# Scores of the first batch: one product of 64 rows per head, masks of a unit ahead of its products

## The chip, the core and the metric

The kernel runs on one core of a Trainium2 chip. TensorE (PE, with its weight loads shown apart as PEld), VectorE (DVE), ScalarE (ACT), GpSimd (POOL) and SyncE (SP, which issues the transfers) run side by side and wait for each other by semaphores. The metric is the device time of one execution in microseconds; several executions of a kernel are given by their median.

## What is computed

Sparse attention over 4 batches and 8 heads, then two feed-forward blocks with a softmax-like layer in the second. Only the attention's scores are touched here:

```python
scores = scale * np.matmul(q, k.transpose(0, 1, 3, 2))         # B, H, S, D = 4, 8, 576, 64
mask_local = (rel >= 0) & (rel < 32)                           # heads 0 to 3
mask_strided = (rel >= 0) & (pos[None, :] % 32 == pos[:, None] % 32)   # heads 4 to 7
scores = np.where(masks[None, :, :, :], scores, -1e9)
attn = softmax(scores); x = attn @ v                           # then x (2304 x 512) goes on:
h = x @ w_in; g = P(h) / (Q(h) + 1e-6); x = g @ w_out          # first block, 2048 wide
h = x @ w_in2; ...; out = ln @ w_out2                          # second block, 1024 wide
```

## The kernel before

**Units.** The attention of one batch is cut into 12 units of two heads each. Units 0 to 5 are local (blocks of 96 queries by 127 keys, two blocks per unit), units 6 to 11 strided (blocks of 126 x 126, 108 x 108 and, in units 8 and 11, a single 108 x 108). A unit has a score product and a mask product for each block of each head: 4 of each, or 2. The two heads of a pair lie one above the other in a tile `qkb`: head 0 of the pair in rows 0 to 63, head 1 in rows 64 to 127. The keys stand there twice, once with zeros in the other head's rows, so that a product over all 128 rows gives one head's scores. For the first batch the third and fourth pair lie in `ws` and `wo_l` (lines of `load_qk`).

**A score.** `scores_head` first adds the mask as a bfloat16 product with the identity (`ident_b`, `mask_b`; it starts the accumulation) and then the float32 product of queries and keys on top. In the first batch (`attn_scores2`) a unit has one PSUM bank for each head: even units `bank0` and `bank1`, odd units the two halves of the pair `banks4`. Later batches (`attn_scores1`) put both heads into one bank, with the same `scores_head`.

**After the scores** come, for a unit, two maxima on DVE (`attn_softmax`), four exponentials on ACT (`attn_exp`), the sum and reciprocal on DVE, the scaling on POOL (`attn_norm`), four transposes on PE (`attn_tp`), an eviction on ACT, the products with V (`attn_pv`: one head writes output rows 0 to 63, the other 64 to 127, so each uses half of the columns of TensorE; the four products of a unit are recorded and mostly stand in the order first head, first head, second head, second head, but in one unit of a later batch, at 251 and 255 us, the planner has put the two heads' products apart, two and two), and the split of the result into two float16 parts, `xs` or `tail`, on ACT and DVE.

**Beside it** run the weight conversions. `w_in` and `w_out` come as 64-bit floats in 8 chunks of 1 MB each; DVE turns a chunk into float32 with three integer instructions on 128 x 1024 elements (`w_conv`), ACT squares it for a scale, PE sums the squares (`ssq`), and ACT and DVE split it into two float16 parts (`w_split`: `wi_h`, `wi_l`, `wo_h`, `wo_l`). When all of `w_in` is converted, `w_pmax` gives `pmax_wi`, and `g_scale` works out the scales of the first block (`pg`, `ih`, `ac`) in some 15 small POOL instructions; the first block's element work (`A`, `p`, `q`, `L`) waits for these.

**What sets the order.** All instructions are recorded, and `Order` lays them out: every engine's instructions get one fixed order, by a planner that goes by costs (`cost`) and due times, over the whole kernel at once. In `cost`, a float32 product with 64 output rows counts half of one with more. All instructions are issued in `emit`, so the profile gives nearly all of them line L413, and they are told apart by their tiles.

Of the kernel before, what the change touches and what calls it, by code (L numbers as in the profile page):

```python
# [17 lines left out]
STRIDE = 32  # L18
# [6 lines left out]
LQ = 96  # L25
LW = LQ + STRIDE - 1
NLB = S // LQ
TPR = S // STRIDE
RG = [7, 7, 6, 6, 6]
RS = [0, 7, 14, 20, 26]  # L30
NSG = len(RG)
QP = S + STRIDE
# [79 lines left out]
class Order:  # L112
# [86 lines left out]
    def cost(self, op):  # L199
        def size(x):  # L200
            n = 1
            for d in x.shape[1:]:
                n *= d
            return n
# [3 lines left out]
        out = (op.outs or op.ins)[0][1]  # L208
        n = max([size(out)] + [size(x) for _, x in ins])
        op.port, op.land = False, 0.0  # L210
        if op.eng == "PE":
            f32 = op.ins[-1][1].dtype == F32
            op.t = size(out) / 2400 + 0.0025
            if op.call == "transpose":
                op.t = 2 * op.t
            elif f32:
                op.t = 2 * size(out) / 2400 + 0.055 if out.shape[0] == 64 else 4 * op.t + 0.03
            op.work = size(out) * op.ins[0][1].shape[0] * out.shape[0] / 16384 * ((2 if op.call == "transpose" else 4) if f32 else 1)
        elif op.eng == "ACT":
            op.t = 0.08 + n * 0.00088 + (0.05 if psum else 0) + (0.09 if "accum_out" in op.k else 0)  # L220
            op.t += 0.08 if n > 300 and hasattr(op.k.get("bias"), "shape") else 0
            op.t = max(op.t, 0.11)
        elif op.eng == "DVE":
            sb = [x for b, x in ins if not b]
            two = op.call in ("scalar_tensor_tensor", "tensor_tensor")
            fast = not two and not psum and op.call == "tensor_scalar"
            op.t = 0.07 + n / (1900 if fast else 960) + (0.08 if "accum_out" in op.k else 0)
            op.t += 0.06 * sum(1 for b, x in op.ins if size(x) == 1)
            op.port = n >= 8 and (len(sb) >= 2 if two else fast)
        elif op.eng == "POOL":  # L230
            two = op.call == "tensor_tensor"
            h = two and out.dtype == F16
            op.t = 0.1 + n * (0.002 if h else 0.0022 if two else 0.00125 if op.call == "tensor_scalar" else 0.001)
            op.t += 0.1 if op.call == "tensor_scalar" and n < 32 else 0
            op.port = bool(ins)
        else:
            op.t = 0.55
            rows, run = min(x.shape[0] for _, x in op.ins + op.outs), min(x.ap[-1][1] for _, x in op.ins + op.outs)
            op.land = n * self.SIZE[out.dtype] * out.shape[0] / (170e3 if op.call != "dma_start" else 240e3 if rows == 64 else 300e3 if run <= 128 else 375e3) * 1.12
# [177 lines left out]
def kernel(ctx: ExitStack, tc: tile.TileContext, qk, v, w_in, w_out, ab, w_in2, w_out2, gln, out):  # L417
# [240 lines left out]
    def unit_info(u):  # L658
        if u < 6:
            p, j = divmod(u, 3)  # L660
            return p, True, [2 * j, 2 * j + 1]
        p, j = divmod(u - 6, 3)
        return 2 + p, False, [[0, 1], [2, 3], [4]][j]

    def blk_dims(local, i):
        if local:
            return LQ, LW
        n = RG[i] * TPR
        return n, n

    at = {}

    def mask_of(local, i, nq, nk):
        return mask_b[0:nq, 2 if not local else 0 if i == 0 else 1, 0:nk]
# [12 lines left out]
    def attn_scores2(b, u):  # L687
        if u % 2 == 0:
            at[b, u] = [psum("h", bufs=2), psum("h", bufs=2)]
        else:  # L690
            t = psum("y", (128, 1024))
            at[b, u] = [t[:, 0:512], t[:, 512:1024]]
        for hh in range(2):
            scores_head(b, u, hh, at[b, u][hh], 0)

    def attn_scores1(b, u):
        t = psum("a", bufs=2)
# [719 lines left out]
```

## Time and profile before

| | us |
|---|---|
| median of 3 runs | 756.23 |
| lowest, highest | 755.44, 756.89 |
| the profiled execution | 757.08 |
| its span | 755.3 |

| engine | busy share of the span | instructions |
|---|---|---|
| PE | 93% | 5406 |
| DVE | 72% | 1114 |
| ACT | 65% | 1155 |
| POOL | 47% | 380 |

The profiled execution is 0.85 us above the median, and 1.8 us of it lie outside its span. The busy shares are means over two very different parts: the first 130 us, in which the weights are converted and the first batch's attention is made, and the rest, in which PE has hardly a gap. The chain that ended last is 84% PE by its share of the span. TensorE's clock has two levels, 1.2 and 2.4 GHz; the granted clock is given as 0.50 or 1.00.

### The profile page before, as it was taken

Reading aid. Unit: us, or ns where it says so; the run is one execution under the profiler, and the core shown is the slowest. Engines: PE = TensorE matmul, PEld = TensorE weight load, DVE = VectorE, ACT = ScalarE, POOL = GpSimd, SP = SyncE. Lnnn points to the kernel's source line nnn. Section 1 sums busy time; section 2 is a strip of 40 time slices with the busy share of each in tenths; the row PEclk is TensorE's granted clock in tenths of the full one; section 3 lists DMA queues with packets and bytes.
Section 4 is the critical chain, followed back from the end, with each engine's and each line's share of the span. In section 5 each row is a group of like instructions: output and inputs, shape, how many; then the busy total and the mean of one; then the engine's idle time right before and its main releaser. Section 6 shows DMA issues by size and latency. Waiting matters only on the chain.

```text
span 755.3 us, 14378 instructions
## 1 busy us (share of the span) xinstructions
PE 699.9 (93%) x5406; PEld 531.7 (70%) x5406; DVE 547.1 (72%) x1114; ACT 489.8 (65%) x1155; POOL 353.0 (47%) x380
## 2 busy tenths in 40 slices
PE   3975368999999999999999999999999999999997
PEld 3763256898888888787777777777776776765443
DVE  6789899689968997787775577576565766644571
ACT  2787558869789679977766676465655646533451
POOL 3233659755689667776434343533534334320000
PEclk9575569999999999999999999999999999999999
DMA  9996801133421321303202010110201011011244
GB/s 270 312 273 167 223 1 34 35 131 127 132 65 60 117 72 34 83 16 62 62 15 43 1 43 1 44 33 10 43 1 43 21 23 43 1 43 43 56 78 103
DMA packets 68101, 55.98 MB, mean 74 GB/s; under 512 B 39616, under 2 KB 56000, under 8 KB 67520
## 3 DMA queue, kind: packets, MB, share of 16 engines
q1 hardware_dynamic: 68032, 55.07, 28.1%
q8 instruction: 42, 0.69, 0.4%
q14 instruction: 27, 0.22, 0.1%
HBM read 40.90 MB, written 4.72 MB: 60 GB/s over the span
## 4 chain that ended last, share of the span: by engine, by line
PE 84%; DVE 7%; ACT 3%; POOL 2%; issue 2%; DMA 1%; SPq 0%; ACTq 0%; DVEq 0%
PE bank L413 46%; PE banks L413 38%; POOL tiny L413 2%; DMA qkb<-in_qk_dram 1%; DVE tiny L413 1%; DVE wi_l L413 1%; DVE T L413 1%; DVE gtb L413 1%; DVE wo_l L413 1%; ACT e L413 1%; DVE p L413 1%; ACT p L413 1%; ACT wo_h L413 0%; DVE bank L413 0%; ACT ysb L413 0%
## 5 line engine op out<-in xcount | busy, mean ns | idle before, releaser
L413 PE MATMUL bank<-xs,wi_h 128*128 128x256 f16 x1152 | 200.0, 278 | 4.0 <-DVE xs L413 2.5
L413 PE MATMUL bank<-xs,wi_l 128*128 128x256 f16 x576 | 159.9, 278 | 1.3 <-DVE wi_l L413 1.3
L413 PE MATMUL banks<-gtb,wo_h 128*128 128x256 f16 x896 | 151.4, 273 | 0.9 <-ACT ysb L413 0.9
L413 PEld LDWEIGHTS <-wi_h 128*128 128x128 f16 x1248 | 124.2, 100 | 30.7 <-issue 4.1
L413 PEld LDWEIGHTS <-wo_h 128*128 128x128 f16 x1152 | 111.7, 98 | 22.1 <-issue 0.9
L413 POOL TENSOR_SCALAR q<-A,aba 128x512 f32<-128x512 f32 x72 | 66.2, 919 | 129.4 <-ACT A L413 129.2
L413 PE MATMUL banks<-gtb,wo_l 128*128 128x256 f16 x448 | 122.1, 273 | 1.7 <-ACT ysb L413 1.7
L413 DVE SCALAR_TENSOR_TENSOR p<-p,ac,bank 128x512 f32<-128x512 f32 x144 | 106.5, 744 | 3.1 <-ACT A L413 0.7
L413 POOL TENSOR_TENSOR gtb<-p,gtb 128x512 f16<-128x512 f32 x56 | 66.8, 1194 | 75.2 <-ACT gtb L413 75.2
L413 DVE TENSOR_TENSOR p<-p,bank 128x512 f32<-128x512 f32 x72 | 49.2, 684 | 69.2 <-ACT p L413 68.7
L413 POOL TENSOR_TENSOR q<-q,A 128x512 f32<-128x512 f32 x72 | 91.7, 1273 | 4.3
L413 PE MATMUL banks<-wi_h,ysb 128*128 128x512 f16 x288 | 90.7, 379 | 0.0
L413 ACT ACTIVATE A<-bank,ih 128x512 f32<-128x512 f32 x72 | 49.6, 689 | 50.8 <-PE bank L413 48.0
L413 DVE SCALAR_TENSOR_TENSOR q<-q,bank 128x512 f32<-128x512 f32 x72 | 49.3, 685 | 34.7 <-ACT bank L413 25.3
L413 PEld LDWEIGHTS <-ysb 128*128 128x128 f16 x432 | 42.1, 98 | 43.8
L413 PE MATMUL bank<-wo_h,T 128*128 128x512 f16 x224 | 70.6, 379 | 0.0
L413 PEld LDWEIGHTS <-wi_l 128*128 128x128 f16 x576 | 57.3, 99 | 12.3 <-issue 3.1
L413 ACT ACTIVATE gtb<-p 128x512 f16<-128x512 f32 x56 | 35.3, 630 | 41.0 <-DVE p L413 41.0
L413 PEld LDWEIGHTS <-wo_l 128*128 128x128 f16 x576 | 56.4, 98 | 7.6 <-issue 0.8
L413 ACT ACTIVATE L<-q 128x512 f32<-128x512 f32 x72 | 45.3, 630 | 24.3 <-POOL q L413 24.0
L413 ACT ACTIVATE p<-bank,ac 128x512 f32<-128x512 f32 x72 | 56.0, 777 | 3.0 <-PE bank L413 3.0
L413 PEld LDWEIGHTS <-T 128*128 128x128 f16 x336 | 32.9, 98 | 34.6
(257 smaller groups left out, 1429.0 us busy)
## 6 DMA issues: line engine op xcount, KB each, us to landing
qkb<-in_qk_dram SPq DMA_DIRECT2D x28, 304.0 KB, 4.6
out_dram<-ot SPq DMA_DIRECT2D x18, 256.0 KB, 2.4
wo_h<-in_w_out_dram SPq DMA_DIRECT2D x4, 1024.0 KB, 5.4
wo_l<-in_w_out_dram SPq DMA_DIRECT2D x4, 1024.0 KB, 7.8
vl<-in_v_dram SPq DMA_DIRECT2D x4, 768.0 KB, 5.1
wi_h<-in_w_in_dram SPq DMA_DIRECT2D x3, 1024.0 KB, 5.4
wi_l<-in_w_in_dram SPq DMA_DIRECT2D x3, 1024.0 KB, 4.9
wo_h<-in_w_in_dram SPq DMA_DIRECT2D x3, 1024.0 KB, 17.3
```

The lines of the kernel that those rows point to most:

```text
L413: getattr(self.real[op.eng], op.call)(*[real(x) for x in op.a], **{k: real(x) for k, x in op.k.items()})
```

## The change

`attn_scores2` no longer calls `scores_head`. It writes the masks of all blocks and both heads of a unit first and then the score products, block by block, the two heads after each other. Each product takes only its head's 64 rows of queries and keys (`t[r, ...]`), so the first head's products use rows 0 to 63 of TensorE and the second head's rows 64 to 127; they write to the two banks that the unit had before. The zeros that made 128-row products possible are still written and loaded. `cost` now also counts a float32 product over 64 rows as half. `attn_scores1`, and with it the later batches, stay as they were in the code.

```diff
-                op.t = 2 * size(out) / 2400 + 0.055 if out.shape[0] == 64 else 4 * op.t + 0.03
+                op.t = 2 * size(out) / 2400 + 0.055 if min(out.shape[0], op.ins[0][1].shape[0]) == 64 else 4 * op.t + 0.03
...
-        for hh in range(2):
-            scores_head(b, u, hh, at[b, u][hh], 0)
+        p, local, ids = unit_info(u)
+        t = qk_t[b, p]
+        nq, nk = blk_dims(local, ids[0])
+        o = [[at[b, u][hh][0:nq, 128 * jj:128 * jj + nk] for hh in range(2)] for jj in range(len(ids))]
+        for jj, i in enumerate(ids):
+            for hh in range(2):
+                PE.matmul(o[jj][hh], lhsT=ident_b[0:nq, 0:nq], rhs=mask_of(local, i, nq, nk), start=(jj == 0), stop=False, skip_group_check=True)
+        for jj, i in enumerate(ids):
+            for hh in range(2):
+                r = slice(64 * hh, 64 * hh + 64)
+                q0 = i * LQ if local else RS[i] * TPR
+                k0 = (1 + hh) * QP + (i * LQ + 1 if local else STRIDE + RS[i] * TPR)
+                PE.matmul(o[jj][hh], lhsT=t[r, q0:q0 + nq], rhs=t[r, k0:k0 + nk], start=False, stop=True, skip_group_check=True)
```

Since the planner orders everything, the order moves on all engines, up to about the middle of the kernel; from there on PE's order (its last 4909 rows) is the same as before. Three places follow.

**PE, the scores of units 0 and 1**, the first of the kernel (`bank0` and `bank1` belong to unit 0, `banks4` to unit 1; `e0`, `ones_f` is a small sum for V). Before:

```order
L413 MATMUL bank2_88<-e0_92,ones_f_78 128x128
L413 MATMUL bank0_86<-qkb0_126 96x127
L413 LDWEIGHTS ident_b_79
L413 MATMUL bank0_86<-mask_b_80,ident_b_79 96x127
L413 MATMUL bank0_86<-qkb0_126 96x127
L413 MATMUL bank1_87<-qkb0_126 96x127
L413 LDWEIGHTS ident_b_79
L413 MATMUL bank1_87<-mask_b_80,ident_b_79 96x127
L413 MATMUL bank1_87<-qkb0_126 96x127
```

Now:

```order
L413 MATMUL bank2_88<-e0_92,ones_f_78 128x128
L413 MATMUL bank0_86<-qkb0_126 96x127 x2
L413 MATMUL bank1_87<-qkb0_126 96x127 x2
L413 MATMUL banks4_90<-qkb0_126 96x127 x4
L413 LDWEIGHTS ident_b_79
L413 MATMUL bank0_86<-mask_b_80,ident_b_79 96x127
```

All eight masks of the two units now stand ahead of the small sum, and the eight products follow each other, by head in twos.

**PE, unit 4** (`bank0`, `bank1`) with what lies between (`bank3` takes transposes, `ident`; `vl` marks the products with V). Before:

```order
L413 MATMUL bank0_86<-qkb1_127 96x127
L413 LDWEIGHTS ident_b_79
L413 MATMUL bank0_86<-mask_b_80,ident_b_79 96x127
L413 MATMUL bank0_86<-qkb1_127 96x127
L413 LDWEIGHTS ident_b_79
L413 MATMUL bank1_87<-mask_b_80,ident_b_79 96x127
L413 MATMUL bank1_87<-qkb1_127 96x127
L413 MATMUL bank3_89<-q1_98,vl0_111 64x96 x4
L413 MATMUL bank2_88<-ident_77,p2_96 127x96 x4
```

Now:

```order
L413 MATMUL bank0_86<-mask_b_80,ident_b_79 96x127
L413 MATMUL bank0_86<-qkb1_127 96x127
L413 MATMUL bank2_88<-q0_97,vl0_111 64x96 x4
L413 MATMUL bank0_86<-qkb1_127 96x127
L413 LDWEIGHTS ident_b_79
L413 MATMUL bank1_87<-mask_b_80,ident_b_79 96x127
L413 MATMUL bank3_89<-ident_77,p1_95 127x96 x3
L413 LDWEIGHTS ident_b_79
L413 MATMUL bank1_87<-mask_b_80,ident_b_79 96x127
L413 MATMUL bank1_87<-qkb1_127 96x127 x2
L413 MATMUL bank3_89<-ident_77,p1_95 127x96
```

The two heads' products of the unit no longer stand together: products with V, masks and transposes have come between them. So it is in most units: from unit 3 on the 32 score products stand in 20 separate pieces, and in one piece alone are both heads.

**DVE, around the instruction `pg0` that waits for the POOL work of `g_scale`**, and `p0`, the first element work of the first block. Before:

```order
L413 TENSOR_SCALAR pg0_136<-tiny_113 128x1
L413 SCALAR_TENSOR_TENSOR wi_l_68<-wo_l_70,scl_wi_116,wi_h_67 128x4x256
L413 TENSOR_SCALAR tiny_113<-pg0_136 128x1
L413 TENSOR_REDUCE tiny_113<-vs0_112 128x1
L413 TENSOR_REDUCE gm2_85<-bank2_88 128x1
L413 TENSOR_TENSOR tiny_113<-tiny_113 128x1
L413 TENSOR_SCALAR pat_wo_115<-bank3_89 128x2
L413 TENSOR_SCALAR gb0_138<-tiny_113 128x1
L413 TENSOR_SCALAR scl_wo_117<-pat_wo_115 128x2
L413 TENSOR_TENSOR gm2_85<-gm2_85 128x1
L413 TENSOR_TENSOR p0_94<-p0_94,bank0_86 128x512
L413 SCALAR_TENSOR_TENSOR wo_l_70<-T1_103,scl_wo_117,wo_h_69 128x16x64
```

Now:

```order
L413 SCALAR_TENSOR_TENSOR wi_l_68<-wo_l_70,scl_wi_116,wi_h_67 128x4x256
L413 TENSOR_SCALAR pg0_136<-tiny_113 128x1
L413 TENSOR_SCALAR inv_wi_118<-pat_wi_114 128x8
L413 TENSOR_SCALAR tiny_113<-pg0_136 128x1
L413 TENSOR_REDUCE tiny_113<-vs0_112 128x1
L413 TENSOR_REDUCE gm2_85<-bank3_89 128x1
L413 SCALAR_TENSOR_TENSOR wo_l_70<-T1_103,scl_wo_117,wo_h_69 128x16x64
L413 SCALAR_TENSOR_TENSOR wo_l_70<-T0_102,scl_wo_117,wo_h_69 128x16x64
L413 TENSOR_TENSOR tiny_113<-tiny_113 128x1
L413 TENSOR_SCALAR pat_wo_115<-bank2_88 128x2
L413 TENSOR_TENSOR p0_94<-p0_94,bank0_86 128x512
```

One weight split (into `wi_l`) now stands ahead of `pg0`, and two (into `wo_l`) ahead of `p0`, instead of behind them.

## Rows read from the trace of the kernel before

**Rows 1.** Busy us (instructions) by stretch; granted PE clock, DMA share, GB/s.

```profile
core 0: us, PE busy (x) PEld busy (x) DVE busy (x) ACT busy (x) POOL busy (x), PEclk, DMA share, GB/s
19.40:43.30 23.90, 22.76 (x127) 19.81 (x127) 17.04 (x39) 16.75 (x66) 7.04 (x5) 0.50 1.05 311
43.30:53.50 10.20, 6.69 (x63) 5.42 (x62) 9.46 (x25) 9.73 (x34) 3.24 (x3) 1.00 1.09 246
53.50:97.90 44.40, 21.91 (x107) 14.86 (x108) 41.62 (x75) 27.59 (x60) 20.73 (x22) 0.50 0.71 186
101.30:111.50 10.20, 6.48 (x31) 4.75 (x32) 10.13 (x19) 4.84 (x10) 9.10 (x10) 0.50 0.00 0
131.00:755.00 624.00, 617.11 (x4883) 465.50 (x4883) 433.26 (x887) 404.68 (x916) 288.26 (x297) 1.00 0.20 51
```

**Rows 2.** PE in order of time: start, duration, operation; waits in brackets.

```profile
11.62 0.74 PE L413 MATMUL bank<-qkb 128*96 128x127 f32 x2 [1.04 <-ACT qkb L413]
...
15.75 0.31 PE L413 MATMUL bank<-mask_b,ident_b 96*96 96x127 bf16 x1
...
20.75 0.74 PE L413 MATMUL banks<-qkb 128*96 128x127 f32 x2
21.29 0.31 PE L413 MATMUL banks<-mask_b,ident_b 96*96 96x127 bf16 x1
21.39 1.10 PE L413 MATMUL banks<-qkb 128*96 128x127 f32 x4
...
30.18 0.31 PE L413 MATMUL banks<-mask_b,ident_b 96*96 96x127 bf16 x1
30.29 0.68 PE L413 MATMUL banks<-qkb 128*96 128x127 f32 x2
30.77 0.31 PE L413 MATMUL banks<-mask_b,ident_b 96*96 96x127 bf16 x1
31.01 0.91 PE L413 MATMUL bank<-q,vl 127*64 127x96 f32 x8
31.85 1.17 PE L413 MATMUL bank<-ident,p 96*127 96x96 f32 x4
...
43.15 0.46 PE L413 MATMUL bank<-ws 128*108 128x108 f32 x2
...
52.07 0.40 PE L413 MATMUL banks<-wo_l 128*108 128x108 f32 x2
```

**Rows 3.** PE later on, at 2.4 GHz: the products with V of three pieces.

```profile
244.30 0.56 PE L413 MATMUL bank<-pts,vl 127*64 127x96 f32 x8
...
251.47 0.55 PE L413 MATMUL bank<-pts,vl 127*64 127x96 f32 x4
...
254.67 0.54 PE L413 MATMUL bank<-pts,vl 127*64 127x96 f32 x4
```

**Rows 4.** ACT in order of time: second head pair scaled, first element work.

```profile
20.02 0.68 ACT L413 ACTIVATE qkb<-qkb 128x576 f32<-128x576 f32 x1
...
84.37 0.69 ACT L413 ACTIVATE A<-bank,ih 128x512 f32<-128x512 f32 x1 [1.35 <-POOL ih L413]
```

**Rows 5.** What DVE waited for between 12.5 and 48 us: total, times, longest.

```profile
DVE tiny L413 <- PE banks L413: 3.9, 7, 1.7
DVE tiny L413 <- PE bank L413: 2.2, 3, 1.5
DVE tiny L413 <- ACT p L413: 2.1, 2, 1.8
DVE pat_wi L413 <- PE bank L413: 0.7, 1, 0.7
```

**Rows 6.** DVE in order of time, unit 11's maximum, then around pg and p.

```profile
56.02 0.26 DVE L413 TENSOR_REDUCE tiny<-banks 108x1 f32<-108x108 f32 x1
...
80.48 0.17 DVE L413 RECIPROCAL tiny<-tiny 128x2 f32<-128x2 f32 x1 [0.16 <-POOL tiny L413]
...
82.93 0.15 DVE L413 TENSOR_SCALAR pg<-tiny 128x1 int32<-128x1 int32 x1 [1.01 <-POOL tiny L413]
83.00 1.28 DVE L413 SCALAR_TENSOR_TENSOR wi_l<-wo_l,scl_wi,wi_h 128x1024 f16<-128x1024 f32 x1
...
87.83 0.69 DVE L413 TENSOR_TENSOR p<-p,bank 128x512 f32<-128x512 f32 x1 [1.50 <-ACT p L413]
88.44 2.48 DVE L413 SCALAR_TENSOR_TENSOR wo_l<-T,scl_wo,wo_h 128x1024 f16<-128x1024 f32 x2
```

**Rows 7.** POOL in order of time, the work of g_scale.

```profile
71.24 9.05 POOL L413 TENSOR_SCALAR tiny<-tiny,aba 128x1 f32<-128x1 f32 x3
...
82.59 0.31 POOL L413 TENSOR_SCALAR tiny<-tiny,aba 128x1 f32<-128x1 f32 x1
```

**Rows 8.** PE in order of time, the last long waits ahead of the full stretch.

```profile
101.89 0.59 PE L413 MATMUL bank<-ssq_wo,ones_f 128*128 128x2 f32 x2 [2.77 <-ACT e L413]
105.61 0.26 PE L413 MATMUL bank<-mask_b,ident_b 96*96 96x127 bf16 x1 [3.13 <-DVE vmax L413]
```

**Rows 9.** Page, transfers: count, KB each, median us from issue to landing.

```profile
wo_h<-in_w_in_dram SPq DMA_DIRECT2D x3, 1024.0 KB, 17.3
```

## What was predicted

> **What bounds the kernel now.** I read the stretches by busy time first, then PE in order of time, then what DVE and PE waited for. From 131 us on PE has 617.11 us of work in 624 [rows 1], at the full clock, and its order from the middle on is unchanged; nothing that the change does can be gained there. The question is when PE comes into that stretch. Ahead of it the bound changes. From 19.4 to 43.3 us PE is busy for 22.76 of 23.90 us at a granted clock of 0.50, while DVE has 17.04 of work [rows 1], and what DVE waits for is mostly PE's scores: 3.9 + 2.2 us of its waits up to 48 us end with a bank that PE filled, 2.1 with exponentials on ACT, 0.7 with a sum for the weight scales [rows 5]. From 53.5 to 97.9 us DVE is the bound, 41.62 of 44.40 us, with PE busy for half the time [rows 1]. DVE's waits there are few: 0.16, 1.01 and 1.50 us around the scales of the first block [rows 6]. The last long waits of PE stand at 101.89 and 105.61, 2.77 and 3.13 us; the second is released by a maximum on DVE [rows 8]. So the change pays through DVE: fewer waits for scores before 48 us, or a better order later.
>
> **The price of a product.** At 1.2 GHz a float32 product over 128 rows comes every 0.59 us with its mask (30.18 to 30.77), of which 0.11 are the mask (30.18 to 30.29). A second product without a mask between costs 0.42 (four passes last 1.10, two last 0.68) [rows 2]. So putting masks first saves 0.06 a product.
>
> **What 64 rows bring** is not in the trace, but its twin is: the products with V use half of the columns, one half per head. A piece with both heads, eight passes, takes 0.56 us; a piece of four passes of one head takes 0.55 and 0.54 [rows 3]. Two heads side by side cost what one costs, and one head alone gains nothing. The bounds of a 64-row product are therefore 0.42 us alone and 0.21 in a pair; I take these by what stands beside it in the new order, not by the planner's half.
>
> In that piece the passes overlap although the program has first head, first head, second head, second head. The Trainium skill says otherwise (TensorE: Matmul & The Clock Gate, Part 3, The mechanism): matrix products start and end in strict program order. By that rule only the two passes at a border between the heads would overlap; the first eight products would take 2.7 us instead of 1.7, and the later sum would be 0.2 more. The trace does not agree: by it one head's four passes and both heads' eight last equally long.
>
> **What a change of shape costs.** From a mask to the products with V it is 0.24 us (30.77 to 31.01) instead of 0.11, so 0.13 to go in. The group lasts 0.84 (31.01 to 31.85) [rows 2], its four products in pairs should take 0.64 (0.42 x 96/127 = 0.32, twice), so 0.20 more for its first product and going out. I take 0.33 for a visit, the nearest row, for half of the rows too; the bounds are nothing and 0.33.
>
> **The sum, part by part.**
>
> 1. Units 0 and 1. Eight products from 11.62 to 15.75 become four pairs: 1.7 + 0.3 = 2.0 instead of 4.1 us, and their masks are done before. Worth 0 at the end: unit 3's products need the second pair's queries, which ACT scales from 20.02 on [rows 4], and they begin at 20.75 [rows 2]. That cover is the transfer; without it 2 us would be gained on PE.
>
> 2. Units 3 to 11, from 20.75 on. 32 products with their masks were 32 x 0.59 = 18.9. Now 32 x (0.42 + 0.11) = 17.0, plus 20 visits x 0.33 = 6.6, less 0.4 for the one pair that meets, less 6 x 0.13 = 0.8 for visits that border on products with V: 22.4. PE has 3.5 us more to do at 1.2 GHz, 2.4 of it up to unit 8 (22 products, 14 visits). Before, PE also waited there twice for about 0.5; the new order fills that. For DVE I count both ways: units 4 to 6 follow with fewer interruptions by the first units' transposes, units 7 to 11 are later. DVE has other work in its queue behind most of those maxima, and a weight split now stands among them. I take +0.5 us, from -1 to +3.
>
> 3. DVE from 80 to 90 us. The split into `wi_l` (1.28) now stands ahead of the wait for `pg`, the two into `wo_l` (2.48) ahead of that for `p` [rows 6]. These waits were 1.01 and 1.50, with 0.16 before. If the splits cover them whole, -2.7; if POOL only becomes later by the same, 0: its three small instructions at 71.24 took 9.05 us while DVE was full, one at 82.59 0.31 [rows 7], so a split in front of the wait can hold POOL up. ACT's halves of the splits also come first. I take -2.0.
>
> 4. PE from 101.89 to 105.61. The maximum that ended the 3.13 us [rows 8] now stands ahead of three splits on DVE. What is late next are sums of `w_out` and element work, and DVE and ACT stay nearly full. I take -0.5, from -3 to 0.
>
> 5. Transfers. The queue of SP keeps its order of loads up to `w_out`; a chunk of `w_in` lands 17.3 us after its issue [rows 9], so DVE can't run far ahead. Nothing, with a loss of up to 1 when the last units' scores free `wo_l` later. The later batches' code is the same, and their order is only reshuffled: 0, within 1.
>
> Net -2.0: 757.08 - 2.0 = 755.1 for an execution like the profiled one, which stood 0.85 above the median: **754.2**. The bounds of its own parts make 752.5 to 756.3.
>
> **The rivals.**
>
> *Slower: half the clock where it was full.* From 43.3 to 53.5 us PE had the full clock, after a stretch of dense 128-row products, and 6.69 us of work [rows 1]. With half the rows, and transposes and products with V between them, the clock may stay at 1.2 GHz. That work then takes up to 6.7 us more, and with part 2 unit 11's scores end at 57.5 to 59 instead of 52.5 (52.07 and 0.40 [rows 2]). The maximum of unit 11 on DVE came at 56.02 [rows 6], so some 3.5 us are covered; beyond that DVE waits, with the conversions of the last `w_in` chunks behind it, and `pmax_wi`, the POOL chain and the first block's work wait for those. Price: 1.5 to 3 in place of the 0.5 of part 2, and half of part 3 lost: +2.5, 758.7 us (757 to 761). For it: PE was nearly full from 19.4 to 43.3 at 0.50 all the same, so a busy PE alone does not bring the clock. Against it: DVE's own work fills much of that time.
>
> *Nothing reaches the end.* POOL delays `pg` and `p` by what the splits take, and parts 2 and 4 cancel: 756.2, within 1.
>
> *The halves overlap everywhere, and a visit costs nothing.* If the two row halves run beside masks and transposes too, the 6.6 us go, and the waits for scores of rows 5 go with them, up to 6.1; the landing of the chunks leaves perhaps 4.5 beyond the forecast: 749.7 (748.5 to 752). The 0.13 into the products with V speaks against it.
>
> *The change does not do what it says*: by the order, 10 of 44 products find a partner. That is part of the forecast, and the reason why it is small.
>
> **How the numbers follow.** Forecast 0.45, slower rival 0.25, nothing 0.17, overlap everywhere 0.13. About 0.2% (1.5 us) is what a measurement of this kernel can tell from no change: faster means below 754.7, slower above 757.7. The forecast has its likeliest time half a microsecond below the first of these; I give 0.28 of its 0.45 to faster, 0.16 to no difference and 0.01 to slower. The slower rival gives 0.20 and 0.05 to no difference; nothing 0.02, 0.13 and 0.02; overlap 0.13 to faster. Sums: faster 0.43, same 0.34, slower 0.23. The range 750.5 to 759.0 leaves out half of the overlap case and the upper third of the slower one, under 0.2 in all. Since both signs are held, the forecast's own range stands beside it: 752.5 to 756.3.
>
> **What the profile after would show.** Eight products of units 0 and 1 in about 2 us with passes in pairs, and unit 3 still at about 20.7 (part 1). Pieces of one head at 0.42 a product, with 0.13 and more before and after (part 2); unit 8's scores 1 to 2 us later than 43.6 (43.15 and 0.46 [rows 2]). DVE's waits at `pg` and `p` gone or short, and the first block's `A` not later than 84.37 [rows 4] (part 3). PE's wait at 105.61 shorter, and the full stretch some 2 us earlier. Wrong would be: the clock at 0.50 through 43 to 53 us with DVE waiting for units 9 to 11 (slower); pieces of one head at 0.21 a product, or no 0.13 (faster).

## The result, and the profile after

| | us, median (lowest to highest) |
|---|---|
| before | 756.56 (755.44 to 759.08, 4 runs) |
| after | 764.58 (763.96 to 764.92, 4 runs) |
| ratio | 1.0089, 95% interval 1.0061 to 1.0116 |
| the profiled execution of after, its span | 763.96, 762.0 |

The change makes the kernel 0.9% slower: 8.0 us, outside the predicted range of 750.5 to 759.0 and away from the forecast of 754.2. About two thirds of that are the half rows themselves. Their price on TensorE I had nearly right and then let vanish behind DVE; with the clock that they cost I had them as a rival, at half of the size. The last third I had put at nothing: the new order of the later batches.

Two stretches of [rows 1] in after, in the same columns, and one more:

```profile
19.40:43.30 23.90, 23.53 (x113) 17.91 (x113) 15.60 (x35) 16.33 (x60) 7.85 (x6) 1.00 1.05 311
43.30:53.50 10.20, 9.05 (x46) 6.82 (x45) 7.92 (x20) 8.31 (x26) 2.69 (x2) 1.00 0.95 201
111.50:124.40 12.90, 7.94 (x52) 6.27 (x51) 12.90 (x28) 11.11 (x18) 12.34 (x15) 0.74 0.03 6
```

The PEclk of 1.00 in the first two rows is no reading. The clock's record of this execution begins only at 83 us, and what lies before it is printed as 1.00. The level there is read from durations: four transposes of 96 columns take 1.17 us at 20.44, and a unit's products with V 0.91 at 44.40, as they did at 0.50 before (31.85 and 31.01) [rows 2]; at 2.4 GHz the products with V took 0.56 [rows 3]. So PE worked at 1.2 GHz through the whole of the first two rows, and was busy for 32.58 of 34.10 us.

PE of after in order of time, as in [rows 2]: the eight products of units 0 and 1, unit 3, unit 8, unit 11, then two waits of many after 100 us:

```profile
11.18 1.17 PE L413 MATMUL bank<-qkb 64*96 64x127 f32 x8 [0.98 <-ACT qkb L413]
12.13 1.16 PE L413 MATMUL banks<-qkb 64*96 64x127 f32 x8
...
19.77 0.73 PE L413 MATMUL banks<-qkb 64*96 64x127 f32 x2 [2.52 <-ACT qkb L413]
20.44 1.17 PE L413 MATMUL bank<-ident,p 96*127 96x96 f32 x4
...
43.78 0.69 PE L413 MATMUL bank<-ws 64*108 64x108 f32 x2
44.40 0.91 PE L413 MATMUL bank<-q,vl 127*64 127x96 f32 x8
...
58.72 0.69 PE L413 MATMUL banks<-wo_l 64*108 64x108 f32 x2
...
118.14 0.59 PE L413 MATMUL bank<-ssq_wo,ones_f 128*128 128x2 f32 x2 [2.01 <-ACT wo_h L413]
...
304.27 0.38 PE L413 MATMUL bank<-xs,wi_h 128*128 128x256 f16 x2 [1.48 <-DVE p L413]
```

The first eight products go in pairs: sixteen passes from 11.18 to about 13.1 us (the second unit's start 0.95 us after the first's), where before the products and the masks between them took 4.1. Unit 11's last score ends at 59.4 instead of 52.5. What DVE waited for from 12.5 to 48 us, as in [rows 5], and after them unit 11's last maximum and `pmax_wi`:

```profile
DVE tiny L413 <- PE banks L413: 5.7, 3, 2.4
DVE tiny L413 <- PE bank L413: 2.5, 3, 1.3
```

```profile
63.35 0.25 DVE L413 TENSOR_REDUCE tiny<-banks 108x1 f32<-108x108 f32 x1
...
75.49 0.14 DVE L413 TENSOR_SCALAR pmax_wi<-tiny 128x1 f32<-128x1 f32 x1
...
84.67 1.28 DVE L413 SCALAR_TENSOR_TENSOR wi_l<-wo_l,scl_wi,wi_h 128x1024 f16<-128x1024 f32 x1
87.04 0.15 DVE L413 TENSOR_SCALAR pg<-tiny 128x1 int32<-128x1 int32 x1 [1.09 <-POOL tiny L413]
```

The same maximum and `pmax_wi` in before, and then the first `A` in after:

```profile
57.32 0.25 DVE L413 TENSOR_REDUCE tiny<-banks 108x1 f32<-108x108 f32 x1
...
70.64 0.14 DVE L413 TENSOR_SCALAR pmax_wi<-tiny 128x1 f32<-128x1 f32 x1
```

```profile
87.68 0.69 ACT L413 ACTIVATE A<-bank,ih 128x512 f32<-128x512 f32 x1
```

DVE's waits for banks grow from 6.1 us [rows 5] to 8.2 up to 48 us, and to 9.8 up to 62 us, where before none were added. Unit 11's last maximum came at 57.32 before and comes at 63.35, `pmax_wi` at 75.49 instead of 70.64, the first `A` at 87.68 instead of 84.37 [rows 4]. DVE did not wait for that last maximum, whose score had ended 3.9 us earlier (59.4): it was late already, by its waits for the units ahead. More is lost later. Two stretches of before, with the columns of [rows 1]:

```profile
111.50:124.40 12.90, 10.60 (x95) 8.76 (x94) 12.73 (x25) 10.21 (x30) 11.16 (x13) 1.00 0.12 30
131.00:450.00 319.00, 318.00 (x2793) 261.78 (x2793) 251.50 (x546) 249.79 (x648) 197.76 (x214) 1.00 0.23 65
```

and the second of them in after:

```profile
131.00:450.00 319.00, 314.57 (x2775) 259.09 (x2774) 248.98 (x538) 247.70 (x643) 202.60 (x213) 1.00 0.24 63
```

From 131 to 450 us PE now has 4.4 us of gaps where it had 1.0, and the clock that came for good at 111.5 us comes at 124.4.

### The profile page after: what moved, and what is told of

It is laid out like the page before. It is cut to its first block, busy times and chain, and to the rows that moved or that the text cites. A ratio compares the mean times of both kernels' runs of the same rounds, so it can differ in the third digit from the quotient of the medians.

```text
span 762.0 us, 14374 instructions
## 1 busy us (share of the span) xinstructions
PE 710.7 (93%) x5406; PEld 535.4 (70%) x5406; DVE 548.6 (72%) x1114; ACT 492.0 (65%) x1155; POOL 363.6 (48%) x380
## 4 chain that ended last, share of the span: by engine, by line
PE 86%; DVE 6%; ACT 3%; DMA 2%; POOL 1%; issue 1%; SPq 1%; ACTq 0%; DVEq 0%
PE bank L413 47%; PE banks L413 38%; DMA qkb<-in_qk_dram 2%; POOL tiny L413 1%; DVE p L413 1%; DVE wo_l L413 1%; DVE T L413 1%; DVE gtb L413 1%; DVE tiny L413 1%; ACT ysb L413 1%; SPq L413 1%; DVE wi_l L413 1%; DVE xs L413 0%; ACT e L413 0%; ACT wi_h L413 0%
## 5 line engine op out<-in xcount | busy, mean ns | idle before, releaser
L413 POOL TENSOR_SCALAR q<-A,aba 128x512 f32<-128x512 f32 x72 | 64.1, 890 | 130.7 <-ACT A L413 130.4
```

The lines of the kernel that those rows point to most:

```text
L413: getattr(self.real[op.eng], op.call)(*[real(x) for x in op.a], **{k: real(x) for k, x in op.k.items()})
```

## The experiments

Each was run beside the kernel before, whose median there was 756.4 to 756.6, and 758.7 once (beside the kernels with repeated masks). Read them for two questions: what do the half rows cost, and what does the new order cost? In the first group the order of all engines is kept, instruction for instruction, and only the product is exchanged.

**Before's order, half rows.** The recorded product stays as it was, so the planner does the same; what is issued is the half.

```diff
+            op = PE.matmul(oo, lhsT=t[:, q0:q0 + nq], rhs=t[:, k0:k0 + nk], ...)
+            if b == 0:
+                r = slice(64 * hh, 64 * hh + 64)
+                op.k.update(lhsT=t[r, q0:q0 + nq], rhs=t[r, k0:k0 + nk])
```

> The order of the kernel before on every engine, instruction for instruction, with each product of the first batch over its head's 64 rows. Each product stands right behind its mask, which takes 96 or more rows, so each of the 44 is a change in and out. Theory 'rows': 44 x 0.35 = 15 us more PE work at 1.2 GHz ahead of 60 us, of which PE's waits there hide a few: 764 to 772. Theory 'order': within 2 us of before, 755 to 758.

769.45 us, ratio 1.0156 (1.0118 to 1.0193). PE of this kernel in order of time:

```profile
31.19 0.34 PE L413 MATMUL banks<-mask_b,ident_b 96*96 96x127 bf16 x1
31.46 0.73 PE L413 MATMUL banks<-qkb 64*96 64x127 f32 x2
32.12 0.34 PE L413 MATMUL banks<-mask_b,ident_b 96*96 96x127 bf16 x1
...
34.17 1.17 PE L413 MATMUL bank<-ident,p 96*127 96x96 f32 x4
```

Mask and product repeat every 0.93 us (31.19 to 32.12); with 128 rows they repeated every 0.59 [rows 2]. A half-row product between full-row work costs 0.34 us more than a full one, which is the 0.33 of the prediction. `A` comes at 96.86 us, 12.5 later than before, and that difference stands unchanged to the end. The 44 visits are worth 44 x 0.34 = 15 us on PE. The 12.5 are not theirs alone, though: no change of the clock is recorded in this execution before 109 us, so the full clock that before had from 43.3 to 53.5 us [rows 1] is gone too, and no run tells the two apart in this order.

**After's order, 128 rows.** The same in reverse, on the changed kernel.

> The changed kernel's order on every engine, instruction for instruction, but each score product over all 128 rows again. Theory 'rows' (the price is that of the 64-row products themselves: going in and out of half rows, some 0.35 us for each of about 22 pieces at 1.2 GHz, and the clock that comes back at 124 us instead of 111): almost all of the 8.0 us is gained back, 756 to 758 us, unit 11's scores end at about 53 us, the full stretch's clock is back at about 112 us. Theory 'order' (the price is that of the new order, in which maxima, transposes and splits stand elsewhere): 762 to 765, unit 11's scores still at 56 or later. In both, the first eight products take about 3.4 us instead of 2.

783.78 us. This says nothing on the rows. PE waited once, for a transfer:

```profile
15.97 0.41 PE L413 MATMUL bank<-qkb 128*96 128x127 f32 x2
45.08 0.74 PE L413 MATMUL bank<-qkb 128*96 128x127 f32 x2 [28.71 <-DMA qkb<-in_qk_dram]
```

The last product of unit 2 belongs to the second head. Over 128 rows it also reads the first head's rows (against zeros), and in the changed order these are already the target of the next batch's load. Half rows had made that order possible. The next kernel keeps half rows in units 2 and 5, the last readers of a pair:

> The changed kernel's order, with products over 128 rows in all units but 2 and 5 (the last readers of a pair's tile, whose second head's products must not touch the first head's rows, since those are reloaded for the next batch first). Against the changed kernel this takes away 24 or more of the half-row products and leaves every order. Theory 'order': the early delay (first element work A at 87.7 instead of 84.4) and the 3.3 us of new gaps after 131 us both stay, 763 to 766. Theory 'rows': the gaps after 131 us stay, the early 3.7 us go, 760 to 762.

758.18 us (756.09 to 761.70), ratio 1.0022 (0.9997 to 1.0047). Exchanging the rows in the changed order gives back 6.4 of the 8 us, so theory "order" falls as the main cause. The time is below the range of theory "rows" as well: in the profiled execution `A` comes at 80.4 us, earlier even than in before. That the later gaps stay, as both theories had it, holds: PE is busy for 314.22 of the 319 us from 131 to 450 us, as in after. And the ten runs fall into two groups, six up to 759.2 and four from 761.0 to 761.7; the experiments on the clock, below, bear on that.

**Other orders.** Does any new order cost? Four kernels: masks first with full rows (the planner counts them in full and makes its own order), the change with the product counted in full, and the kernel before with one number of the planner moved by a hair.

```diff
-                op.t = ... else 4 * op.t + 0.03
+                op.t = ... else 4 * op.t + 0.031        (reshuffle_a)
-    EARLY, PEARLY, SLACK = 0.1, ...
+    EARLY, PEARLY, SLACK = 0.101, ...                   (reshuffle_b)
```

> Only the first half of the change: the masks of a unit first, the products still over 128 rows and counted by the planner in full, so its own new order. Theory 'rows': 755 to 758, as before or a little better, since four to eight changes of weights less. Theory 'order' (any reordering by the planner costs): 760 to 765.

> The change as it is, with products of 64 rows and masks first, but the planner counts each as it counted a product of 128 rows, in time and in work. The order is a third one. Theory 'rows': 762 to 768, as the changed kernel, since the pieces are still apart. Theory 'the planner's count' (it takes 0.16 us for a product that takes 0.42 alone, and so puts work behind the scores that comes too early): 755 to 758.

> The kernel before with one number of the planner changed: a float32 product is counted 0.001 us longer. No instruction differs; the order does, on all engines. Theory 'any new order costs' (the order before is a picked one of many): 760 to 766, with one to five us of new gaps after 131 us. Theory 'only masks first and half rows cost': 755 to 758.

> The kernel before with another number of the planner changed, the early start that it grants between engines from 0.100 to 0.101 us. No instruction differs. Theory 'any new order costs': 760 to 766. Theory 'only masks first and half rows cost': 755 to 758.

| kernel | us | ratio (95%) | PE busy of the 319 us from 131 to 450 us |
|---|---|---|---|
| masks_first_128 | 763.50 | 1.0078 (1.0054 to 1.0103) | 313.50 |
| old_cost_work | 765.38 | 1.0106 (1.0061 to 1.0151) | 315.22 |
| reshuffle_a | 758.16 | 1.0017 (1.0000 to 1.0034) | 316.18 |
| reshuffle_b | 758.71 | 1.0025 (1.0008 to 1.0043) | 317.30 |

The two reorderings without any changed instruction cost about 0.2%, and for one of them the interval reaches down to nothing; their times lie between the ranges of both theories. The masks alone, without a half row, cost nearly as much as the whole change: 4.5 us of new gaps of PE after 131 us, and a wait of PE of 5.11 us for `p` at 115.51. So an order can lose 7 us by itself, and both theories had been too simple. The planner's count of the product is not the fault: counted in full, the kernel is no faster than the changed one.

**The later order by itself.** The next two take the planner's order up to its time 150 (about 139 us on the chip), and from there the order of before, written into the kernel as a list; PSUM banks are dealt out anew along the joined order. One has 128 rows (units 2 and 5 excepted), one is the changed kernel with all its half rows.

```diff
+        return self.forced(seq, LATE, 150.0)      # seq: the new order; LATE: the old one
```

> The changed kernel's order with 128 rows (all but units 2 and 5) up to about 139 us, where PE stands 4.1 us ahead of the kernel before, and from there the order of before, written into the kernel as a list. Theory 'the new order's later part gives back its gain' (3.3 us of new gaps of PE between 150 and 310 us): these gaps go, and the kernel is 2.5 to 4 us faster than before, 752.5 to 754. If the gaps come because ACT and DVE are behind with work that the early order put off, they come back elsewhere: 755 to 757.

> The changed kernel as it is (half rows everywhere, its own order) up to about 139 us, and from there the order of before. Theory 'two terms that add': the gaps after 131 us fall from 4.8 us to about 1 and the time by 3.5 to 4 us, 760.5 to 761.5, with A still at 87.7. If the later gaps come from the late start and not from the order, they stay and the time is 763 to 765.

755.67 us (752.13 to 757.66), ratio 0.9987 (0.9968 to 1.0005), and 760.80 us (760.34 to 761.32), ratio 1.0049 (1.0028 to 1.0070). The rows of both from 131 to 450 us, the full-row one first, with the columns of [rows 1]:

```profile
131.00:450.00 319.00, 318.11 (x2798) 261.99 (x2797) 250.41 (x543) 248.88 (x648) 195.60 (x212) 1.00 0.24 65
```

```profile
131.00:450.00 319.00, 318.10 (x2807) 262.89 (x2807) 250.77 (x544) 249.37 (x651) 197.71 (x213) 1.00 0.24 65
```

With the later order of before the gaps are gone in both: 3.5 us of PE time, and 764.58 - 760.80 = 3.8 us of the kernel's. A late start does not bring them, the order does. With half rows and the later order taken apart, the 8 us read:

| from | to | us |
|---|---|---|
| before, 756.4 | new early order, 128 rows: 755.7 | -0.7 (not told from none) |
| 755.7 | the same with half rows: 760.8 | +5.1 |
| 760.8 | with the new later order, after: 764.6 | +3.8 |

The two terms do not quite add. With the new later order the half rows cost 764.58 - 758.18 = 6.4 us, and with full rows the later order costs 758.18 - 755.67 = 2.5. So the half rows stand at 5.1 to 6.4 us and the later order at 2.5 to 3.8. (The full-row kernels keep half rows in units 2 and 5.)

**What the half rows cost at one clock, and the clock.** The profiled execution of the full-row kernel (new_then_old) took 757.66 us. The same kernel was profiled again:

> The kernel with the changed order to 139 us and products over 128 rows, nothing changed. Its first profile was a run of 757.7 us at 1.2 GHz up to 60 us, with A at 84.4. Theory 'clock': a run of 752 to 755.5 shows the full clock for ten or more us between 20 and 50 us, and A at 80.5 to 82.5; a run of 757 to 758 shows none.

753.99 us. From 23 to 43 us, in the columns of [rows 1], first the execution of 757.66 us, then this one, each followed by its first `A` on ACT:

```profile
23.00:43.00 20.00, 20.00 (x115) 16.84 (x113) 15.22 (x34) 15.16 (x56) 5.81 (x4) 1.00 1.06 298
...
84.38 0.69 ACT L622 ACTIVATE A<-bank,ih 128x512 f32<-128x512 f32 x1
```

```profile
23.00:43.00 20.00, 14.80 (x133) 12.12 (x132) 18.80 (x45) 17.92 (x66) 7.13 (x5) 0.93 1.05 293
...
81.42 0.69 ACT L622 ACTIVATE A<-bank,ih 128x512 f32<-128x512 f32 x1
```

It is the same program with the same order. In the second execution the granted clock is full for nearly all of the stretch (0.93); in the first there is no record (1.00 again), and its four transposes take 1.17 us at 34.92, against 0.60 at 35.84 in the second, so it ran at 1.2 GHz. The clock gives PE slack, DVE 18.80 us of work in place of 15.22, and the kernel 757.66 - 753.99 = 3.7 us. That such a kernel's runs form two groups is then the clock's coming or not; of twelve runs seven lay up to 756.1 and five from 757.2 on. The mean granted clock of every run, over its whole span, sorts them nearly the same way. Time ahead of the first record counts as 1.00 in it, so a run whose clock first changes late reads high: 0.968 in the execution of 757.66 us, where the first change comes at 54 us. The seven lower runs have 0.952 to 0.961, like the second profile (0.957); four of the five upper ones have 0.968 to 0.970, and one 0.943.

The half-row kernel (after_then_old) shows the early clock in none of its seven runs: their times lie within 1 us, and their mean granted clocks are 0.982 to 0.993, where the profiled one (0.982) has its first change at 84 us. The changed kernel's four runs have 0.982 to 0.991. Against the full-row execution at 1.2 GHz after_then_old loses 760.80 - 757.66 = 3.1 us. Unit 11's last score on PE and last maximum on DVE, first with full rows, then with half rows:

```profile
54.74 0.40 PE L622 MATMUL banks<-wo_l 128*108 128x108 f32 x2
...
60.05 0.25 DVE L622 TENSOR_REDUCE tiny<-banks 108x1 f32<-108x108 f32 x1
```

```profile
59.26 0.69 PE L622 MATMUL banks<-wo_l 64*108 64x108 f32 x2
...
63.88 0.25 DVE L622 TENSOR_REDUCE tiny<-banks 108x1 f32<-108x108 f32 x1
```

PE ends 4.8 us later (55.14 to 59.95), the maximum comes 3.8 us later, and the first `A` 88.17 - 84.38 = 3.8. From DVE's maximum to `A` nothing of the delay is absorbed, and 3.1 of it reach the end.

**Is it the half rows that keep the clock away, or the idle time ahead?** Three kernels fill PE's waits for the first transfers with repeated masks (a repeat overwrites the same values).

```diff
+TIMES = {0: 14, 1: 14, 3: 13}          # before_warm: {0: 15, 1: 15}
...
+                for _ in range(getattr(op, "times", 1)):
                     getattr(self.real[op.eng], op.call)(...)
```

> The changed kernel, with the first masks of units 0 and 1 made 14 times instead of once and those of unit 3 13 times (each repeat overwrites the same values), in the time in which PE waits for transfers (3.4 to 9.4 and 16.9 to 19.8 us). Theory 'half rows keep the clock away': the repeats may bring the full clock for a few us, but it is gone again by 25 us and the time is as the changed kernel's, 763.5 to 766. Theory 'PE's idle stretches keep it away': full clock from about 20 us on, 758 to 761.

> The same repeats in the kernel with the changed order to 139 us, products over 128 rows and the later order of before. Its runs came in two groups, 752.1 to 756.1 and 757.2 to 757.7. Theory 'the clock decides, and dense work on PE brings it': all runs fall in the lower group, 752 to 755. Theory 'the clock comes by chance': two groups as before, median 755 to 757.

> The kernel before, with the first masks of units 0 and 1 made 15 times in the time in which PE waits for the first transfers (3 to 9 us). Theory 'dense work brings the clock': full clock from before 16 us into the stretch that stood at 1.2 GHz from 19.4 to 43.3 us, PE no longer full there, DVE's waits for scores shorter, 752.5 to 755. Theory 'by chance': 755.5 to 760 as before.

764.45 us, 756.90 and 757.76; ratios 1.0088 (1.0065 to 1.0111), 0.9992 (0.9977 to 1.0006), 1.0003 (0.9986 to 1.0020). PE of after_warm and then of new_then_old_warm, behind the same 28 masks:

```profile
16.32 3.22 PE L417 MATMUL banks<-mask_b,ident_b 96*96 96x127 bf16 x28
19.47 0.74 PE L417 MATMUL banks<-qkb 64*96 64x127 f32 x2
20.14 1.17 PE L417 MATMUL bank<-ident,p 96*127 96x96 f32 x4
...
23.38 0.92 PE L417 MATMUL bank<-q,vl 127*64 127x96 f32 x8
```

```profile
17.21 3.15 PE L626 MATMUL banks<-mask_b,ident_b 96*96 96x127 bf16 x28
20.15 0.69 PE L626 MATMUL banks<-qkb 128*96 128x127 f32 x2
20.62 1.01 PE L626 MATMUL bank<-ident,p 96*127 96x96 f32 x4
...
23.31 0.56 PE L626 MATMUL bank<-q,vl 127*64 127x96 f32 x8
```

The order is the same, and PE is dense in both. With full rows the clock comes (0.56 us for the products with V, and 0.88 granted from 20 to 33 us); with half rows it does not (0.92, and the first change is recorded at 98 us), and the time is the changed kernel's. In the three other runs of after_warm the mean granted clock is 0.935, so it changed early there too; their times are the same all the same, 763.77 to 764.84. PE's idle time ahead is therefore not what keeps the kernel slow. One pair of executions would not settle the rest, since full rows too run at 1.2 GHz in some; what speaks for the half rows is that none of the eleven runs of after and after_then_old shows the early clock, and that with full rows in the same order about half do. Why half rows keep it away stays open.

What the repeats do not do is make a faster kernel: in new_then_old_warm the full clock is gone again from 30 to 37 us and from 43.5 to 98 us, and that execution's `A` is at 84.48. In before_warm sixty masks follow each other from 2.67 us on, and there the masks alone brought the clock:

```profile
2.67 3.36 PE L417 MATMUL banks<-mask_b,ident_b 96*96 96x127 bf16 x30 [2.67 <-POOL mask_b L417]
5.83 2.13 PE L417 MATMUL bank<-mask_b,ident_b 96*96 96x127 bf16 x30
```

The full clock is recorded from 6.4 us on, and it falls at 9.9, after PE has waited; in the profiled executions of the other two kernels sixty masks from 2.67 to about 9.2 us left it at 1.2 GHz. The clock must come at the right time, and for long enough.

The kernel before was profiled again too, for its own upper group:

> The kernel before, nothing changed. If it falls in its upper group (about 759.5 to 760.5), theory 'clock' expects no full clock from 43 to 53 us there, and the first element work A some 3 us later than 84.4; in its lower group (about 756) the profile should be as the one shown.

756.36 us, the lower group, with the full clock from about 43 us as in [rows 1] (0.89 over 40 to 50 us). What its upper runs look like was not profiled. Beside the experiments 107 runs of before are on record: the 39 from 758.2 us on have a mean granted clock of 0.946 on average, the 68 up to 757.2 us 0.951. That would be some 9 us less of the full clock, an estimate from these means; but single runs overlap (0.938 to 0.955 and 0.947 to 0.958), so it stays open.

**Where half rows are cheapest, and where they hurt.** In before's order six units (0, 1, 2, 7, 10, 11) stand together on PE. There the masks were put first and the heads in turn, with half rows and with full ones; all else is before's order.

> The order of before on all engines, except inside six units of the first batch (0, 1, 2, 7, 10 and 11) whose instructions already stand together on PE: there the masks come first and the products are of 64 rows, the heads in turn, so that all 22 find a partner. Nothing else moves. Theory 'order' (half rows are good where they meet, the price was the new order): 754 to 756.5, with shorter waits of DVE for scores up to 62 us. Theory 'rows' (the clock of 43 to 53 us is lost with half rows, and every unit pays a way in): 757 to 760.

> The order of before with the six regrouped units (masks first, heads in turn), but products over all 128 rows. Against the same with half rows (0.1% slower than before, no full clock between 43 and 53 us, pairs of products in 0.42 us): here a product takes 0.42 us alone, and PE should have the full clock from 43 us. Theory 'clock': within 1 us of the kernel before, 755 to 757, and at least as fast as with half rows, though each pair takes twice as long at 1.2 GHz. Theory 'no price of half rows where they meet': 1 to 2 us slower than with half rows.

758.67 us, ratio 1.0012 (0.9992 to 1.0032), and 756.01, ratio 0.9994 (0.9975 to 1.0013). Unit 7 and a later piece, with half rows and then with full ones:

```profile
38.72 1.06 PE L428 MATMUL banks<-ws 64*108 64x108 f32 x8
39.71 0.33 PE L428 MATMUL bank<-mask_b,ident_b 108*108 108x108 bf16 x1
...
44.00 0.92 PE L428 MATMUL bank<-q,vl 127*64 127x96 f32 x8
```

```profile
38.70 1.74 PE L428 MATMUL banks<-ws 128*108 128x108 f32 x8
40.22 0.30 PE L428 MATMUL bank<-mask_b,ident_b 108*108 108x108 bf16 x1
...
43.83 0.56 PE L428 MATMUL bank<-q,vl 127*64 127x96 f32 x8
```

Where the heads meet, the halves do what the change wants: four products in 0.99 us (38.72 to 39.71) instead of 1.52 (38.70 to 40.22), the way in and out included. The clock takes it back: at 44 us PE is at 1.2 GHz with half rows and at the full clock without. Even with all 22 products of these units in pairs the half rows gain nothing. (Two of the ten half-row runs lay at 755.4 and 755.7, the others from 758.1 up. The mean granted clock is 0.959 and 0.957 in those two, about as in the lower runs of before; in seven of the others it is 0.984 to 0.995, and 0.984 belongs to the profiled execution, whose first change comes at 80 us. One has 0.950. With full rows all twelve have 0.946 to 0.954. So half rows in six units seem to let the early clock through at times, and the two runs that had it were the fastest.)

Last, the changed order with half rows in the local units alone, or in the strided ones (and 2 and 5) alone:

> The changed kernel's order, with half rows only in units 0 to 5 (as far as about 34 us) and products over 128 rows in units 6 to 11. Against the same order with 128 rows nearly everywhere (first element work A at 80.4 us, PE's full clock from about 23 us to 43 us) and the changed kernel (A at 87.7, 1.2 GHz to 83 us). Theory 'clock' (most of the 7.3 us between them is the full clock that half rows keep away): no full clock up to about 34 us, then it comes with the 128-row units, A at 83 to 86. Theory 'visits' (most is the 0.35 us for each way in and out): the loss is shared by the number of visits, 12 of 20 here, A at 84.5 to 85.

> The changed kernel's order, with half rows only in units 2, 5 and 6 to 11, and products over 128 rows in units 0, 1, 3 and 4. Theory 'clock': the full clock comes at about 23 us as with 128 rows and falls back when units 6 to 11 come (about 30 us), so that half of the 7.3 us is lost, A at 83 to 85. If half rows do not take the clock away, the full clock stays to 43 us, each visit costs half as much, and A is at 81 to 82.

760.91 us, ratio 1.0051 (1.0031 to 1.0071), and 762.69, ratio 1.0074 (1.0050 to 1.0099). The local one in the columns of [rows 1]:

```profile
20.00:40.00 20.00, 20.00 (x113) 15.77 (x113) 13.14 (x32) 14.48 (x56) 7.01 (x5) 1.00 1.05 319
40.00:50.00 10.00, 7.09 (x50) 6.20 (x49) 9.74 (x23) 9.79 (x29) 2.69 (x2) 0.73 1.10 236
50.00:60.00 10.00, 5.37 (x47) 4.17 (x47) 9.51 (x25) 8.93 (x34) 2.87 (x3) 0.84 0.98 270
```

As long as units 0 to 5 run, PE is full and no change of the clock is recorded; when the full-row units follow, the full clock comes (first recorded at 37.8 us; 0.73 and 0.84), and `A` is at 83.17. That is what theory "clock" expected. Of the strided one the profiled execution took 2473.68 us and is not read, so what was expected of its `A` stays open. Its other runs lie in two groups, four from 760.6 to 761.3 us with a mean granted clock of 0.944 to 0.951, and three from 764.1 to 765.2 with 0.993, 0.940 and 0.993.

## Why the prediction was wrong, step by step

- **What bounds the kernel.** Right in outline: PE's scores up to some 50 us, DVE from there, PE from 131. What the outline left out is that DVE, once it is the bound, hands on whatever it was late by: 3.8 us at unit 11's maximum are 3.8 at `A` and 3.1 at the end.
- **Part 1, units 0 and 1, worth 0.** Right: eight products in about 2 us, in pairs. Unit 3 follows at 19.77, still released by the scaled queries on ACT, which come 1 us earlier than the 20.02 of [rows 4]. What this part is worth at the end no run measures by itself. The Trainium skill's strict program order (TensorE: Matmul & The Clock Gate, Part 3, The mechanism) would have made it 2.7 us by the prediction's estimate; the passes of both heads ran together, and it was 1.9.
- **The price of a visit, 0.33.** Right: 0.34 in the order of before. The Trainium skill names a cause (TensorEngine Tiling (Array Packing), Key Properties): changing the tiling mode, and not only the tile, drains TensorE. It gives no price, and no run here shows the drain itself; the 0.34 us stand in the trace.
- **Part 2, +3.5 us on PE, taken as +0.5 at the end.** This is the first step that failed. PE's part was near: with the rows alone exchanged, at one clock, unit 11's last score ends 4.8 us later, where the same sum gives 22.4 - 17.0 = 5.4 (unit 5, one of its nine units, has half rows in both kernels). "DVE has other work in its queue behind most of those maxima" was wrong: 3.8 us of the 4.8 reach unit 11's maximum and `A`, and 3.1 the end, where I took 0.5. I had seen one cover, DVE's weight work, and not asked how much of it was left when the maxima came late; the waits of DVE for banks say it (6.1 to 9.8 us up to 62 us).
- **The slower rival, half the clock where it was full.** The mechanism was right, and its sign stood in the profile: 1.2 GHz through 43 to 53 us, and DVE waiting for a bank again after 48 us. Its size was not. I priced it at 2.5 in all, part 2 included. Even that was counted from the wrong place: its own terms (2.25 in place of the 0.5 of part 2, half of part 3's -2.0, and part 4's -0.5) lie some 2.75 above the forecast, which is 0.75 above before, 757.0 us and not 758.7. Measured are 5.1, of which 3.1 are part 2 at one clock and 2.0 a clock that full rows get in about half of the runs and that none of the eleven runs of after and after_then_old shows early. It also reaches further than I thought: not the full clock of 43 to 53 us alone, but any full clock ahead of 83 us. The Trainium skill (TensorE: Matmul & The Clock Gate, Part 1, What's actually happening) has a busy PE release its throttle. Here PE was busy for 23.53 of 23.90 us from 19.4 to 43.3 us with half rows at 1.2 GHz, and in one execution with mostly full rows for 20.00 of 20.00 us from 23 to 43 us, at 1.2 GHz too; being busy was not enough.
- **Part 3, -2.0 around `pg` and `p`.** About right: from `pmax_wi` to `A` it was 84.37 - 70.64 = 13.73 us and is 87.68 - 75.49 = 12.19, so -1.5. The wait for `pg` itself did not shrink, though (1.01 [rows 6] to 1.09): half of the 1.5 lies ahead of `pg` (12.29 to 11.55 from `pmax_wi`), half between it and `A`. The wait for `p` is gone. Why POOL's step came later by as much as the split was not tried.
- **Part 4, -0.5 for the wait at 105.61.** Of the wait for `vmax` 0.25 us are left, and others stand in its place (2.01 for `wo_h` at 118.14 among them). From 111.5 to 124.4 us PE had 7.94 us of work at a mean clock of 0.74, and before 10.60 at 1.00.
- **Part 5, later order "only reshuffled: 0, within 1".** The largest failure: 2.5 to 3.8 us. I took the order of the later batches for a detail because its code is the same. From 131 to 450 us before had 1 us of gaps, which says how good that order was, and so how much a random other one could lose. Masks first with full rows lost 4.5 there, two reorderings without a changed instruction 0.7 to 1.8.
- **The range of its own parts, 752.5 to 756.3.** It does not follow from the parts: their bounds, added up from 756.2, give about 748.5 to 761.2. So wide a sum would have said that the size was not known.
- **"Halves overlap everywhere, a visit costs nothing"** is out: one head alone takes 0.73 us for two passes, a full-row product 0.68 (30.29 [rows 2]), and its neighbours pay.

## A version that beats both?

The joined order with full rows (new_then_old) has the lowest median, 755.67, and single runs down to 752.13; its interval (0.9968 to 1.0005) still holds no change. It beats the changed kernel by about 1% (ratios 1.0089 and 0.9987, each beside its own before), and is not shown to beat the one before. It needs half rows in units 2 and 5 alone, for the order of the loads.

## What to carry to other kernels

Here half rows saved time on TensorE only where the two halves stood side by side, with nothing of another shape between (0.99 us for four products instead of 1.52); a product alone paid the change of shape for nothing, and the clock of all the other work was lost with it. Where a planner sets the order of the whole kernel, a local change is two changes: price the new order too, by how few gaps the old one had, and test the edit in the old order before judging it. When a stage's bound engine has no slack, a delay ahead of it is handed on whole; a cover counts only once its remaining length is known.

## What the runs showed of the hardware

- The granted clock of one program in one order differs from execution to execution: 0.93 from 23 to 43 us in one, 1.2 GHz by its durations in another, 3.7 us apart.
- A PE that is busy with hardly a gap can stay at 1.2 GHz: 23.53 of 23.90 us with half-row scores between masks, transposes and products with V (after, 19.4 to 43.3 us), and 20.00 of 20.00 with mostly full rows in one execution (new_then_old, 23 to 43 us). 76 repeats of masks ahead of the half rows did not make the kernel faster (after_warm).
- Masks alone can bring the full clock or not: of sixty in a row the second thirty took 2.13 us instead of 3.36 (before_warm), while sixty from 2.67 us on, and 28 more for 3.2 us, stayed at 1.2 GHz in after_warm and new_then_old_warm. In the last the clock rose at 23.0 us, with full-row products running since 20.15.
